# Windowed attention into a gated feed-forward block on one core: the third token tile's output product in seven block products, and a scheduler that takes every operation's place from a table

## The chip, the cores and the metric

The kernel runs on one core of one Trainium2 chip. The metric is the device time of one execution in microseconds (us). Before the change it is 309.03 us, the median of three executions (308.63 to 310.61). The profiled execution has a span of 307.2 us from its first instruction to its last.

The core's engines work at the same time, each through its own queue in order: PE multiplies matrices into the eight PSUM banks, ACT and DVE read PSUM and SBUF, POOL works on SBUF alone and issues the loads, and SP issues the stores and some copies.

## The reference, cut to what matters

```python
# q, k, v: (8, 8, 576, 64); window 64, causal
scores = (q @ k^T) / 8, masked to 0 <= i - j < 64
x = (softmax(scores) @ v).transpose(0, 2, 1, 3).reshape(4608, 512)
gate = np.maximum(x @ w_gate, 0.0)        # 512 x 1536
val = x @ w_val                           # 512 x 1536
return ((gate * val) @ w_out).astype(np.float32)   # 1536 x 512
```

## The kernel before, in words

The 4608 tokens are cut into nine tiles of 512 (tiles 0 to 8). Each tile goes through three stages.

**Attention.** For each half of the heads there is one run of 72 small matmuls ("scores", L377 and L385), four exponentials on ACT (L645), then small matmuls with the values ("values", L391), a reciprocal and a scaling on DVE (L660, L398), and a transpose on DVE (L403) that makes the tile's x.

**Hidden layer.** Tile 0 is multiplied with the weights directly (`direct_block`, L750). Tiles 1 to 8 use a scheme with seven block products for eight (`fast_hidden`, L842): the products P1 to P7 on blocks of x, on the weights and on sums of them. Per group of features and per weight (gate or value), the products P1, P6, P7 and P4 add into one and the same PSUM bank, called A, in this order. Between two of them ACT copies the bank's state to SBUF (a "snap", L851); the next product into A starts only after that copy. The copies are later added to the banks B and C by DVE (L858). ACT applies the relu (L867), and POOL multiplies gate and value into `g_sb` (L876).

**Output.** `output` (L900, its matmuls L916) multiplies a tile's `g_sb` with `wo` directly: four pieces of 128 tokens, each with three groups of four matmuls of 512 columns, an ACT copy out of PSUM (L927) and a store. `fast_output` (L955, its matmuls L1005) does it with seven block products of two halves, each half being six matmuls of 256 columns, with four sums of `g_sb` blocks on DVE (L973), three snaps on ACT (L1016), three sums on DVE (L1041) and one copy out (L1044 on ACT). `w_sums` (L939) makes the sums of `wo` blocks that this needs, once, on POOL and DVE (L950). One of its three-part sums overwrites a block of `wo`, so it has to wait for the last direct output. The constant `TF` says which tile is the first to use `fast_output`; it is 3 here, so tiles 0, 1 and 2 are done directly.

**The order of the work.** `first_part` is written out by hand: the loads that come first, 93 idle matmuls (`PADS`), and the attention of most of tile 0. The rest, `second_part`, only lists operations: each with the engines that can do it, an assumed duration, the operations it comes after, the buffers it takes and gives, and a key. `Plan.run` then plays the program through with the assumed durations; whenever an engine is free it takes the ready operation with the lowest key, and emits it. So the order in each engine's queue is settled when the program is built, and each engine then keeps to that order on the chip. The keys come from a table of constants `K` (a period per tile plus offsets per kind of operation and tile).

The plan also counts PE's instructions, since their code is loaded in blocks of 256 (`fetch`, L93): it assumes when a block is asked for and when it is there, and puts off a run of small matmuls that would have to wait for its code. `plan.at` is the count with which `second_part` starts. `fill` (L115) looks for stretches where PE would idle and books filling matmuls there, in the count and by a call of `emit`; `emit` drops what is not an operation, so no such matmul is in the program.

The loads of weights, q, k and v all go through POOL's queue (L337, L340, L347, L356), at most eight of them under way in the plan.

Of the kernel before, what the change touches and what calls it, by code (L numbers as in the profile page):

```python
# [20 lines left out]
K = {"T1": 33.417, "STEP": 29.94, "wo1": 24.303, "wo2": 136.509, "q0": 0.81, "q1": 2.61, "q10": -9.561, "q11": 1.093, "v": -0.6, "v1": 1.142, "ql": 1.41, "qt": 0.88, "qti": 4.69, "vl": 0.91, "vc": 0.04, "vm": 1.83, "e": 7.62, "gap": 3.77, "gap1": -1.003, "r": -6.21, "tn": 1.66, "xf": 4.78, "wf": -1.338, "wfj": 2.6, "sn": 2.67, "su": -2.15, "re": 17.5, "mu": -6.61, "la": -4.79, "o0": 11.594, "o0j": 20.432, "o0s": -4.369, "oo": 0.007, "os": 0.386, "oj": 4.81, "gs": -1.18, "fo": 0.015, "fi": 0.098, "fs": 4.74, "fu": 0.27, "W0": 129.92, "TF": 3, "rs": 7.037, "rv": 3.751, "rt": 4.292, "wl": 1.63, "wln": 5.389, "l0": 0.003, "l1": 4.021, "lv": 1.186, "lvs": 12.368, "wo0": 25.921, "db": -7.955, "di": 1.563, "dv": 0.646, "slack": 0.3, "d2": 3.05, "bl": 9.0, "lv0": 18.364, "d": {'0:q0': 0.808, '0:fs': 1.88, '0:la': 1.692, '1:oo': 0.058, '0:fi': 0.024, '1:qt': 3.036, '1:os': -0.226, '0:vc': -1.15, '0:tn': -0.981, '0:qt': 0.904, '0:e': -2.629, '0:sn': 0.475, '0:vm': 0.58, '0:vl': 0.514, '0:ql': 0.128, '0:fu': -2.028, '1:tn': 3.174, '0:re': 0.858, '1:ql': -1.577, '0:xf': -0.14, '0:su': 0.053, '0:gap': 0.391, '0:r': -2.955, '0:oo': -0.042, '0:os': 0.025, '1:vm': 0.483, '1:fo': -0.017, '0:q1': 0.357, '1:sn': 0.632, '0:oj': -0.104, '0:qti': -0.947, '0:gs': -0.096, '0:fo': -0.029, '2:xf': -3.116, '1:oj': -0.851, '1:fu': -1.619, '1:gs': -1.956, '1:vl': 3.671, '1:fs': -1.692, '1:q0': -0.44, '1:re': 17.838, '1:qti': -0.251, '2:vl': -1.63, '1:xf': 0.54, '2:v': 0.897, '2:e': 3.091, '1:vc': -0.626, '2:gap': 1.519, '1:mu': -1.202, '2:oj': 1.272, '2:os': -0.152, '1:gap': -2.068, '1:su': 1.664, '1:q1': 0.09, '1:la': -0.927, '2:fu': -0.861, '2:q0': -1.678, '2:su': -3.121, '1:v': 0.703, '1:r': 0.099, '2:tn': 0.263, '2:mu': -0.767, '2:qti': -1.435, '2:sn': 0.235, '2:qt': 0.357, '3:re': -0.971, '3:su': 1.85, '2:gs': 0.316, '2:vc': -0.222, '2:fi': 0.018, '3:fs': 2.376, '2:oo': -0.024, '3:gs': -0.499, '2:ql': 2.087, '2:re': 1.781, '2:vm': -0.346, '2:la': -0.408, '3:fo': 0.105, '3:qt': -1.251, '3:qti': -0.756, '3:fi': 0.003, '3:r': 4.605, '4:tn': 4.441, '4:fo': 0.176, '3:sn': 1.86, '3:v': -0.191, '3:gap': 0.067, '3:q1': -1.861, '4:v': -2.381, '3:fu': -1.0, '3:e': -2.398, '3:ql': 0.244, '3:q0': -0.417, '4:ql': 1.859, '4:qti': -0.846, '3:oo': 0.017, '3:oj': -1.455, '3:mu': 5.549, '3:vl': -0.094, '3:la': -1.756, '3:os': 0.07, '4:qt': -2.162, '5:v': 2.345, '5:e': -6.12, '5:gap': -0.396, '4:re': 16.126, '4:r': -3.179, '4:os': 0.054, '4:q0': -0.903, '4:gap': -1.023, '4:fu': -1.144, '5:vm': 1.185, '4:fi': -0.029, '4:vm': 1.023, '4:la': 2.23, '4:vl': 0.037, '5:tn': -1.009, '5:r': -1.653, '5:fu': 0.073, '5:re': 3.794, '4:q1': 1.992, '4:sn': 1.164, '4:xf': -1.831, '5:fi': -0.019, '4:mu': 1.169, '4:oj': 1.089, '5:qti': -1.537, '5:fo': -0.021, '5:xf': -1.396, '5:gs': -0.82, '5:mu': -2.334, '5:vc': -0.566, '5:oo': 0.002, '5:q0': -0.047, '4:vc': 0.378, '5:qt': -1.506, '4:fs': 0.072, '5:ql': -0.361, '5:oj': 0.91, '5:fs': -0.532, '5:q1': -0.028, '4:oo': -0.002, '5:la': 0.275, '6:oo': -0.051, '6:vl': -1.345, '6:v': 0.087, '7:vc': 2.102, '6:os': 0.034, '7:fo': -0.026, '6:tn': -1.475, '6:gap': -1.442, '6:xf': 3.27, '6:fi': -0.035, '6:fo': -0.054, '6:fu': -0.179, '6:qt': 0.741, '7:tn': -0.289, '7:vl': -0.177, '6:ql': -0.604, '7:re': 9.431, '7:fi': 0.019, '7:xf': -0.992, '6:vc': -0.932, '7:sn': -0.018, '6:e': 6.905, '6:q1': 1.236, '7:ql': -0.482, '7:e': -4.862, '7:qt': 1.66, '6:mu': -0.73, '7:gap': 0.823, '6:oj': 0.303, '6:q0': 0.231, '6:r': 2.887, '7:su': 1.478, '7:gs': -0.403, '7:q0': -0.079, '7:q1': -0.303, '7:vm': -1.095, '6:gs': -0.02, '7:mu': -0.49, '7:fs': 1.309, '7:la': -0.048, '7:os': 0.117, '7:qti': -1.407, '7:r': -0.97, '7:fu': -0.866, '6:re': 0.021, '6:la': 0.896, '7:oo': -0.007, '6:sn': 0.915}}  # L21
# [5 lines left out]
class Op:  # L27


    def __init__(self, name, key, engines, fn, after, take, give, dma):  # L30
        self.small = 0
        self.count = 0
        self.opens, self.closes = None, False
        self.name = name
        self.key, self.engines, self.fn = key, engines, fn
        self.take, self.give, self.dma = take, give, dma
        self.left = len(after)
        self.feeds = []
        self.ready = dict.fromkeys(engines, 0.0)
        self.end = None  # L40
        self.on = None


class Plan:
# [12 lines left out]
    def __init__(self, free, queue, pools):  # L57
# [4 lines left out]
        self.taken = {}  # L62
        self.open = []
        self.filled = []
# [50 lines left out]
    def fill(self, o, t, emit):  # L115
        if t - self.free["PE"] < 0.7:
            return
        free = [(self.taken[id(h[n])], h[n]) for pool, h, names in o.take if "bank" in pool for n in names]
        free += [(x[0], x[2]) for pool in ("bank", "bo") for x in self.pools[pool]]
        if free or self.open:  # L120
            since, bank = min(free, key=lambda x: x[0]) if free else (0.0, self.open[-1]["b"])
            since = max(self.free["PE"], since + 0.1)
            n = int((t - 0.25 - since) / 0.165)
            if n > 0:
                self.fetch(2 * n, since, 0.165 * n, True)
                self.filled.append((since, n, t, o.name))
                emit((bank, bool(free)), n)

    def finish(self, o, e, t, dur):
        if e == "PE":  # L130
            if o.opens is not None and o.opens in self.open:
                self.open.remove(o.opens)
            if o.opens is not None and not o.closes:
                self.open.append(o.opens)
# [29 lines left out]
    def grab(self, o, e, t):  # L164
# [7 lines left out]
        for holder, names, items in got:  # L172
            for name, item in zip(names, items):
                self.pools[self.home[id(item[2])]].remove(item)
                self.taken[id(item[2])] = item[0]
# [37 lines left out]
    def run(self, emit):  # L213
# [7 lines left out]
        while left:  # L221
# [7 lines left out]
            while moved:  # L229
                moved = False  # L230
                for e in ("PE", "ACT", "DVE", "POOL", "SP"):
# [13 lines left out]
                    if e == "PE":  # L245
                        self.fill(o, begin, emit)
# [9 lines left out]
def kernel(  # L256
# [255 lines left out]
    def second_part():  # L512
# [562 lines left out]
        def emit(o, e):  # L1075
            if not isinstance(o, Op):
                return
# [46 lines left out]
```

## Time and profile before

| | |
|---|---|
| Time, median of three (lowest to highest) | 309.03 us (308.63 to 310.61) |
| Span of the profiled execution | 307.2 us |
| PE busy | 297.1 us, 97% |
| DVE, POOL, ACT busy | 246.2, 229.8, 213.0 us |
| Granted TensorE clock, mean | 0.999 |
| Matmuls of the direct output (L916) | 144 of 512 columns |
| Matmuls of the seven-product output (L1005) | 504 of 256 columns |

The difference between the median time and the profiled span, 1.83 us, lies outside the first and last instruction. Durations of instructions below are those of this one execution. A matmul's shown end is a modelled one: matmuls follow each other faster than their shown durations. The profile calls an engine's wait "issue" when it ended with nothing that the profile shows.

### The profile page before, as it was taken

What the parts mean: (1) busy time and instruction counts of PE and PEld (TensorE: products, weight loads), DVE (VectorE), ACT (ScalarE), POOL (GpSimd) and SP (SyncE); (2) the same over time, 40 slices, a digit from 0 to 9 for tenths busy, and PEclk for the clock granted to TensorE, in tenths of its full rate; (3) what the DMA queues carried; (4) which work ended last, traced back from release to release, by engine and by line L of the source; (5) the groups of instructions that cost most, each with busy time, mean ns of one, the idle gap of its engine ahead of it and who ended that gap; (6) DMA issues with size and microseconds to landing.
All of it is one profiled execution on the core that took longest, in us unless ns stands there. A gap on an engine that the chain in (4) does not pass through costs nothing.

```text
span 307.2 us, 11254 instructions
## 1 busy us (share of the span) xinstructions
PE 297.1 (97%) x4772; PEld 240.2 (78%) x4772; DVE 246.2 (80%) x422; ACT 213.0 (69%) x414; POOL 229.8 (75%) x233
## 2 busy tenths in 40 slices
PE   7889999998999999999999999999999999999995
PEld 5475845786757886777888888888888888888884
DVE  5858997988963997887989988878896789595762
ACT  4445335897768787788778786778687886878721
POOL 8696957998999899999189954995479157938520
PEclk9999999999999999999999999999999999999999
DMA  7999999983249953996694194674112011201033
GB/s 219 187 190 206 196 194 198 202 169 22 19 78 150 183 99 75 139 182 136 123 72 82 34 165 120 48 166 37 54 36 69 6 38 37 68 0 36 1 121 120
DMA packets 59074, 32.87 MB, mean 107 GB/s; under 512 B 39440, under 2 KB 53392, under 8 KB 59024
## 3 DMA queue, kind: packets, MB, share of 16 engines
q0 software_dynamic: 46672, 18.29, 51.1%
q1 hardware_dynamic: 12208, 13.80, 14.2%
q8 instruction: 37, 0.61, 0.8%
q14 instruction: 13, 0.11, 0.1%
q10 hardware_dynamic: 144, 0.07, 0.1%
HBM read 37.75 MB, written 9.44 MB: 154 GB/s over the span
## 4 chain that ended last, share of the span: by engine, by line
PE 85%; DMA 8%; POOL 3%; issue 2%; DVE 1%; ACT 0%; ACTq 0%; DVEq 0%; POOLq 0%
PE bank L842 48%; PE bank L1005 18%; PE bank L916 8%; PE bank L391 4%; PE bank L750 3%; DMA wo<-in_moe_w_out_dram 3%; DMA wv<-in_moe_w_val_dram 3%; DMA k<-in_k_dram 2%; PE bank L385 2%; PE bank L377 1%; POOL vs L791 1%; POOL v L356 1%; POOL q L347 0%; POOL k L347 0%; DVE xw L398 0%
## 5 line engine op out<-in xcount | busy, mean ns | idle before, releaser
L876 POOL TENSOR_TENSOR g_sb<-pr,pr 128x512 f16<-128x512 f32 x96 | 121.6, 1283 | 47.7 <-ACT pr L889 16.5
L858 DVE TENSOR_TENSOR pr<-bank,pr 128x512 f32<-128x512 f32 x144 | 92.6, 678 | 24.7 <-PE bank L842 21.9
L851 ACT COPY pr<-bank 128x512 f32<-128x512 f32 x144 | 79.9, 590 | 30.2 <-PE bank L842 27.9
L842 PE MATMUL bank<-xt,vs 128*128 128x256 f16 x384 | 56.7, 273 | 0.0
L842 PE MATMUL bank<-xt,us 128*128 128x256 f16 x384 | 56.2, 273 | 0.0
L867 ACT ACTIVATE pr<-pr 128x512 f32<-128x512 f32 x72 | 45.4, 639 | 5.9 <-DVE pr L858 5.5
L842 PE MATMUL bank<-xt,wg 128*128 128x256 f16 x288 | 42.8, 273 | 0.0
L842 PE MATMUL bank<-xt,wv 128*128 128x256 f16 x288 | 42.7, 273 | 0.0
L842 PEld LDWEIGHTS <-us 128*128 128x128 f16 x384 | 37.0, 98 | 6.5 <-issue 0.2
L842 PEld LDWEIGHTS <-vs 128*128 128x128 f16 x384 | 37.2, 98 | 4.7
L645 ACT ACTIVATE p<-bank 128x512 f16<-128x512 f32 (+1 forms) x68 | 35.7, 592 | 6.7 <-PE bank L385 6.5
L916 PE MATMUL bank<-wo,g_sb 128*128 128x512 f16 x144 | 35.9, 380 | 0.3 <-DMA wo<-in_moe_w_out_dram 0.3
L356 POOL DMA_DIRECT2D v<-in_v_dram x40 | 34.9, 883 | 0.5 <-issue 0.5
L889 ACT ACTIVATE pr<-bank 128x512 f32<-128x512 f32 x48 | 27.1, 601 | 6.7 <-PE bank L842 5.0
L842 PEld LDWEIGHTS <-wg 128*128 128x128 f16 x288 | 27.7, 98 | 4.7
L842 PEld LDWEIGHTS <-wv 128*128 128x128 f16 x288 | 28.1, 98 | 4.2
L1005 PEld LDWEIGHTS <-g_sb 128*128 128x128 f16 x288 | 27.9, 98 | 3.4
L1005 PE MATMUL bank<-wo,g_sb 128*128 128x256 f16 x216 | 28.4, 273 | 0.0
L398 DVE TENSOR_TENSOR xw<-bank,r 128x448 f16<-128x448 f32 (+2 forms) x45 | 25.8, 575 | 1.5
L403 DVE STREAM_TRANSPOSE xt<-xw 128x512 f16<-128x512 f16 (+2 forms) x38 | 25.0, 668 | 0.5 <-ACT xw L506 0.3
L1005 PEld LDWEIGHTS <-ss 128*128 128x128 f16 x216 | 21.0, 98 | 2.5
L916 PEld LDWEIGHTS <-g_sb 128*128 128x128 f16 x144 | 13.5, 98 | 11.3 <-issue 0.3
(95 smaller groups left out, 389.4 us busy)
## 6 DMA issues: line engine op xcount, KB each, us to landing
out_dram<-pr SPq DMA_DIRECT2D x35, 256.0 KB, 2.4
k<-in_k_dram POOLq DMA_DIRECT2D x15, 288.0 KB, 7.5
q<-in_q_dram POOLq DMA_DIRECT2D x15, 288.0 KB, 7.1
v<-in_v_dram POOLq DMA_DIRECT2D x32, 128.0 KB, 6.4
v<-v SPq DMA_DIRECT2D x12, 132.0 KB, 2.6
v<-v SPq DMA_DIRECT2D x24, 66.0 KB, 2.3
wg<-in_moe_w_gate_dram POOLq DMA_DIRECT2D x6, 256.0 KB, 6.6
wv<-in_moe_w_val_dram POOLq DMA_DIRECT2D x6, 256.0 KB, 7.9
```

Source lines behind the costliest of these rows:

```text
L356: nc.gpsimd.dma_start(v16s[b % 2][lo:hi, g, :, 0:64], v[b, :, 64 * g - 64 + lo:64 * g - 64 + hi].rearrange("h p d -> p h d"))
L398: nc.vector.tensor_tensor(x, blocks_of(to, n)[:, :, 0:D].rearrange("p s (c e) -> p s e c", e=2), r[:, :, :, None].to_broadcast([128, n, 2, ...
L403: nc.vector.transpose(xt[:, 2 * hh:2 * hh + 2, c0:c0 + n].rearrange("p e (s c) -> p s e c", c=32), x)
L645: nc.scalar.activation(pp[g][:, 0:n].rearrange("p n c -> p (n c)"), st[g][:, 0:64 * n], ACT.Exp, scale=scale)
L842: nc.tensor.matmul(slot[to][:, HT * m:HT * m + HT], w[:, kk, 128 * m:128 * m + 128], x[:, kk], start=(first and m == 0 and kk == 0), stop= ...
L851: lambda e, hold=hold, slot=slot: nc.scalar.copy(hold["x"], slot["A"]),
L858: nc.vector.tensor_tensor(hold["x"], slot[to], hold["x"], ADD)
L867: lambda e: nc.scalar.activation(hold["x"], hold["x"], ACT.Relu), after=[o])
L876: lambda e: VEC[e].tensor_tensor(gh[:, fs:fs + 2, h], pair(a["x"]), pair(b["x"]), MUL),
L889: lambda e, hold=hold, slot=slot, i=i: nc.scalar.activation(hold["x"], slot["A"], ACT.Copy if i else ACT.Relu),
L916: nc.tensor.matmul(bank["b"][:, 0:c1 - c0], gs[t % 2][:, f, 128 * sub:128 * sub + 128], wo[:, f, c0:c1], start=(j == 0 and i == 0), stop=( ...
L1005: nc.tensor.matmul(bank[to][:, HD * m:HD * m + HD], a[:, f, 128 * m:128 * m + 128], b[:, f], start=(first and m == 0 and f == 0), stop=(f ...
```

## The change

`TF` goes from 3 to 2, so tile 2 is done by `fast_output` too, and `w_sums` waits for the direct outputs of two tiles. The durations and start times that the plan assumes are set to new values. `fill` and what it needs are taken out. After all 1618 operations are listed, each one's key is replaced by a number from a table `PLACES`. Everything else in `K` stays; it now matters only for what reads it beside the keys.

```diff
-K = {..., "TF": 3, ...}
+K = {..., "TF": 2, ...}
+PLACES = [int(n) / 100 for n in """
+-1900 -468 778 272 1607 821 1292 824 3602 2123 12645 -290 -1508 6258 ...
...
@@ fetch
-                begin += max(0.4, min(6.5, self.queue["q"] - begin), min(2.0, self.queue["sp"] - begin))
-                come.append(begin + 2.4 + K["slack"])
+                begin += max(0.7, min(4.0, self.queue["q"] - begin), min(2.0, self.queue["sp"] - begin))
+                come.append(begin + 1.2)
...
-    def fill(self, o, t, emit):
-        if t - self.free["PE"] < 0.7:
-            return
...
@@ second_part
-        plan = Plan({"PE": 14.3 - FRONT, "ACT": 16.2 - FRONT, "DVE": 16.8 - FRONT, "POOL": 13.2 - FRONT, "SP": 3.0},
-                    {"q": 16.4 - FRONT, "sp": 3.0},
...
+        plan = Plan({"PE": 15.35, "ACT": 16.95, "DVE": 17.55, "POOL": 13.6, "SP": 3.0},
+                    {"q": 16.6, "sp": 3.0},
...
-        plan.at = 428 + 2 * 72
-        plan.asked, plan.got, plan.come = 2, 1, [12.1 - FRONT, 18.8 - FRONT]
+        plan.at = 428 + 2 * PADS
+        plan.asked, plan.got, plan.come = 2, 1, [7.9, 16.9]
...
-                                        after=[turns[b - 1, name, hh]] if b > 1 else [], dma=(0.59, 0.40, "q"))
+                                        after=[turns[b - 1, name, hh]] if b > 1 else [], dma=(0.59, 0.41, "q"))
...
-                                              dma=(0.26 * (part[2] - part[1]) / 128, 0.22, "q"))
+                                              dma=(0.26 * (part[2] - part[1]) / 128, 0.28, "q"))
...
-            run = op("scores", key, pe(0.0081 * 8 * n + 0.0268 * n), lambda e: score_run([st[g] for g in range(G)], items),
+            run = op("scores", key, pe(0.0083 * 8 * n + 0.0268 * n), lambda e: score_run([st[g] for g in range(G)], items),
...
-            a = op("values", key, pe(0.031 * m), run, after=after, take=[("bank", to, ("b",))], give=gives)
+            a = op("values", key, pe(0.02 + 0.031 * m), run, after=after, take=[("bank", to, ("b",))], give=gives)
...
+                if f0 < 4 and kind == "v" and c0 < 2 * U:
+                    ops[-1].ready["PE"] = 17.95
...
+        assert len(PLACES) == len(plan.all)
+        for o, place in zip(plan.all, PLACES):
+            o.key = place
         end = plan.run(emit)
```

As built, PE's program changes from 144 to 96 matmuls of the direct output and from 504 to 588 of the seven-product output. The other counts that change: ACT 417 to 419 instructions, DVE 424 to 429, POOL 238 in both. The order within every queue changes from the first operation of `second_part` to near the end.

More of the change, by code (lines that the diff above doesn't have):

```diff
@@ L113, in fetch @@
         return t
-    def fill(self, o, t, emit):
-        if t - self.free["PE"] < 0.7:
-            return
[L118 to L127, printed above, removed]
     def finish(self, o, e, t, dur):
         if e == "PE":
[L131 to L134, printed above, removed]
             dur += self.TURN * ((o.small > 0) != self.small)
@@ L920, in output @@
                         before[0].count = 4
-                        before[0].opens, before[0].closes = bank, j == NJ - 1
                         mine += before
```

19 lines of the change are left out of this document (5 added, 14 removed), and 66 rows, old and new, of the table PLACES.

## The prediction

> **What bounds the kernel now.** I read the page first, then the busy time by stretches, then the chain that ended last, then the order of time around each gap on PE.
>
> From the page:
>
> ```profile
> PE 297.1 (97%) x4772; PEld 240.2 (78%) x4772; DVE 246.2 (80%) x422; ACT 213.0 (69%) x414; POOL 229.8 (75%) x233
> PE 85%; DMA 8%; POOL 3%; issue 2%; DVE 1%; ACT 0%; ACTq 0%; DVEq 0%; POOLq 0%
> q8 instruction: 37, 0.61, 0.8%
> ```
>
> PE sets the end: 97% busy, 85% of the chain. So the time falls only by what leaves PE or by what PE waits. Where it waits, by stretches (length, then PE, PEld, DVE, ACT and POOL busy with their instructions, clock, DMA share, GB/s):
>
> ```profile
> 15.00:50.00 35.00, 33.22 (x557) 22.78 (x556) 28.01 (x60) 15.63 (x35) 26.60 (x35) 1.00 1.37 198
> 50.00:150.00 100.00, 98.37 (x1671) 74.88 (x1671) 83.03 (x135) 78.16 (x149) 91.06 (x90) 1.00 0.86 127
> 150.00:303.00 153.00, 153.00 (x2237) 134.82 (x2236) 124.08 (x203) 111.68 (x208) 101.42 (x87) 1.00 0.32 63
> ```
>
> After 150 us PE never stops. Before that it is idle for 1.78 and 1.63 us. Matmul ends are modelled, so I size the gaps from start to start instead. From the chain (start, length, what), the true spacings:
>
> ```profile
> 57.59 0.86 PE bank L916 x4
> 74.65 3.93 PE bank L842 x36
> 176.77 1.31 PE bank L1005 x12
> ```
>
> A 512-column matmul takes 0.86/4 = 0.215 us, a 256-column one 3.93/36 = 1.31/12 = 0.109. The gaps in order of time:
>
> ```profile
> 16.64 0.33 PE L750 MATMUL bank<-xt,wv 128*128 128x192 f16 x2
> 17.97 1.33 PE L750 MATMUL bank<-xt,wv 128*128 128x192 f16 x14 [1.01 <-DMA wv<-in_moe_w_val_dram]
> ...
> 29.67 1.26 PE L750 MATMUL bank<-xt,wg 128*128 128x128 f16 x16 [0.20 <-DVE xt L403]
> ...
> 50.13 1.02 PE L916 MATMUL bank<-wo,g_sb 128*128 128x512 f16 x4 [0.33 <-DMA wo<-in_moe_w_out_dram]
> ...
> 70.31 0.21 PE L391 MATMUL bank<-v,p 128*32 128x65 f16 x3
> ...
> 71.55 0.82 PE L391 MATMUL bank<-v,p 128*32 128x65 f16 x69 [1.03 <-issue]
> ...
> 149.13 0.20 PE L385 MATMUL bank<-qT,kT 32*128 32x64 f16 x2 [0.31 <-issue]
> ```
>
> From start to start, less the stream itself, they are worth: x transposes at 15.1 us, 0.30; the first value weights, 1.17; x transposes at 29.1 and 29.7, 0.57; exponentials at 41.9, 0.40; `wo` at 50.1, 0.52. Together 2.96 us before 50 us. Then 0.52 around 53 and 66 us, 1.24 at 70.3, 0.15 at 94, 0.50 at 148.6: 2.41 us. The two called "issue" I take for PE's code: 9544 PE instructions in blocks of 256 make 37, the packets of queue q8.
>
> **The change part by part.**
>
> *Seven products for eight in tile 2.* Out go 12 groups of four wide matmuls at 0.86: 10.32 us. In come 14 groups of six narrow ones at 0.655: 9.17. PE: **-1.15 us**. DVE gets four block sums (1.11, 0.96, 0.95, 0.95) and three sums at 0.68: +6.0 us, less about 1.0 for value copies that move to ACT and POOL. ACT swaps four copies for three snaps and one copy. This lies beside PE: DVE is busy 83 of 100 us between 50 and 150 us, POOL 91, so 17 and 9 are open. Without that cover, up to 6.0 us of later sums would hold PSUM banks and PE would wait for them. The overwriting sum of `wo` moves from after tile 2's direct outputs to after tile 1's; in the built order 25 groups of the hidden layer alone (25 x 0.437 = 10.9 us) stand on PE between the last of these and the first product that reads it. I cost it at nothing. The stores stay in number and size on SP's queue.
>
> The row above stands against a rule of the Trainium skill, page "TensorE: Matmul & The Clock Gate", section "Back-to-back issue gap": in a sustained stream of weight load and matmul pairs, a 512-column matmul takes about 131 ns and a 128-column one 81. An estimate from that page puts 256 columns near 98 ns, so the exchange would cost 84 x 98 - 48 x 131 ns, some +1.9 us instead of -1.15. The trace's 215 and 109 ns do not agree with it.
>
> *The stretch to 50 us.* In the new order PE runs, behind the first two gate blocks, the small scores (0.47 us) and a third gate block (0.66) before it asks for the value weights. The third block needs x transposed, done at 17.57, so PE starts it near 17.65 and ends at 18.31. By then it has done three blocks and the scores, 2.43 us of work; before, it had done 18.31 - 15.03 less its gaps of 0.30 and 1.17, so 1.81: 0.62 gained. Between tile 0's values and the 128-column blocks that need their transpose now stand four blocks (2.6 us) for two (1.3); the row of DVE steps between took 1.9 (28.07 to 29.94): the 0.57 goes. Between scores and values of tile 1 two more blocks (1.3) stand: the 0.40 goes. That is 1.59. But the last third of `wo` landed at 50.09, behind the same loads. PE would ask for it at 49.61 - 1.59 plus 0.87 of work put ahead of it (28 value matmuls, one product), 48.9. If the landing stays, PE waits 1.2 and only the 0.87 is kept. In POOL's queue five sums of 1.16 stand ahead of that load for seven, so it can be issued up to 2.3 earlier, though its queue serves in order; I take 0.4 earlier: **-1.3** (bounds 0 and -2.96).
>
> *50 to 150 us.* The plan's count of PE instructions starts 42 further on (93 pads for 72), and `fill` no longer books code for matmuls never emitted. Both put its block borders where the program's are, so it can keep small runs off them. I take 0.8 of the 1.74 at "issue" and none of the other gaps: **-1.4** (bounds 0 and -2.41).
>
> *What the new order adds.* One more stretch of small matmuls on PE: +0.1, as one change of kind cost 0.09 before. Then the handing over of bank A: from the last issue of a product to the next one into A pass 0.21 until ACT starts (0.04 behind the shown end, which is 0.17 behind the stream), 0.59 for the copy (L851), 0.04 to release: 0.84. By PE's order and the spacings above, none of the 144 hand-overs before has less than 1.09 of other work between; now three have less than 0.9 (0.44, 0.71, 0.87, all near tile 1's first group), which lacks 0.40 + 0.13. So +0.5. Within 1.2 stand 19 for four. Where ACT is in another copy of 0.59, one that has 1.09 lacks 0.34; 16 x 0.34 = 5.4 is the whole; the four before lost nothing visible. I take an eighth: +0.7 (bounds 0 and 5.4). Behind a waiting product stands everything on PE.
>
> *Sum:* -1.15 - 1.3 - 1.4 + 0.1 + 0.5 + 0.7 = -2.55. On the profiled span 307.2 this gives 304.7; with the 1.83 outside it as in the median, **306.5 us**. The last 3.8 us (last matmul at 303.4, then copy and store) stay.
>
> **The rivals.**
>
> *A, all gaps close.* -1.15 - 2.4 - 2.0 + 0.6 = -4.95: about 304.1; with a part of it, 304.5. For it: every gap before 150 us has a cause that the new figures name (17.95 for the value weights, the count). Against: the `wo` landing and the tight hand-overs.
>
> *B, gaps only move.* `wo` lands as before or later, the code blocks meet other small runs: -1.15 + 0.6, 308.5. For it: loads fill the queue up to 50 us at 198 GB/s, and PE's order cannot hasten them.
>
> *C, slower: the hand-overs of bank A decide.* 19 stand within 1.2 and 37 more within 1.32; with a copy ahead they need 0.84 + 0.59 = 1.43. All hit would be 19 x 0.34 + 37 x 0.12 = 10.9. Two thirds of it, 7.2, against gains of 3.85, gives 309.0 - 3.85 + 0.6 + 7.2 = 313.0. It decides from 3.3 us on, a third of them. For it: PE has not one idle moment after 150 us now, so the new order can only lose there beyond the exchange. Against: ACT is busy 112 of 153 us there.
>
> *D, the exchange does not pay.* If shown durations were the cost (273 ns narrow, 380 wide), 84 x 0.273 - 48 x 0.380 = +4.7 replaces -1.15: 312.4. Against it stand the spacings on the chain. The Trainium skill's 131 ns above would give 309.5, by that page ("TensorE: Matmul & The Clock Gate") alone.
>
> **How the numbers follow.** My forecast 0.42 (own range 305.2 to 308.0), A 0.25, B 0.20, C 0.11, D 0.02. A measurement of this kernel tells about 1% from no change: below 305.9 is faster, above 312.1 slower. A and 0.13 of the forecast make 0.38 faster; half of C and D, 0.06 slower; the rest 0.56. The range 303.8 to 310.2 leaves out the far end of A and C.
>
> **What would show it.** In the output stage 96 matmuls of 0.215 and 588 of 0.109. No gap at the first value weights over 0.6 us, none at the 128-column blocks; the `wo` wait larger than 0.52. Code gaps of 1.24 and 0.50 gone or small. New: short PE waits on ACT's copies in the hidden layer after 150 us. I am wrong if PE stops for more than 3 us after 150 us, if a gap over 1 us stands at a code block again, or if the span falls under 302.

## The result: about 2 us slower

| | before | after |
|---|---|---|
| Time, median of twenty (lowest to highest) | 308.23 us (307.03 to 310.61) | 310.39 us (308.99 to 314.35) |
| Ratio, 95% interval | | 1.0067 (1.0047 to 1.0087) |
| Span of the profiled execution | 307.2 us | 308.0 us |
| That execution's own time | | 309.76 us |
| A second profile of the same kernel: span, own time | 306.5, 308.42 us | 308.3, 309.96 us |

The changed kernel is slower by 0.67%, some 2.07 us. The two spans of before differ by 0.7 us, so the profile that the prediction was made from was one of the longer ones. The mean spans, 306.85 and 308.15, are 1.3 us apart. About half of the rest is that the profiled executions of the changed kernel lie 0.05 and 0.6 us under their medians, and the second of before 0.2 over 308.23.

### The profile page after: what moved, and what is told of

Its sections match the earlier page's. It is cut to its first block, busy times and chain, and to the rows that moved or that the text cites. A ratio compares the mean times of both kernels' runs of the same rounds, so it can differ in the third digit from the quotient of the medians.

```text
span 308.0 us, 11241 instructions
## 1 busy us (share of the span) xinstructions
PE 297.1 (96%) x4808; PEld 244.0 (79%) x4808; DVE 251.9 (82%) x427; ACT 215.7 (70%) x416; POOL 228.8 (74%) x233
## 4 chain that ended last, share of the span: by engine, by line
PE 86%; DMA 7%; DVE 2%; issue 2%; ACT 1%; POOL 1%; SPq 0%; ACTq 0%; POOLq 0%; DVEq 0%
PE bank L888 46%; PE bank L1050 21%; PE bank L962 7%; PE bank L436 4%; DMA v<-in_v_dram 3%; PE bank L430 3%; DMA v<-v 2%; PE bank L422 2%; PE bank L794 2%; DMA vs<-in_k_dram 1%; PE bank L497 1%; DVE us L837 0%; DVE qT L398 0%; DVE kT L398 0%; POOL us L837 0%
## 5 line engine op out<-in xcount | busy, mean ns | idle before, releaser
L904 DVE TENSOR_TENSOR pr<-bank,pr 128x512 f32<-128x512 f32 x144 | 94.1, 683 | 19.6 <-ACT pr L897 9.2
L897 ACT COPY pr<-bank 128x512 f32<-128x512 f32 x144 | 81.3, 587 | 24.1 <-PE bank L888 20.6
L888 PE MATMUL bank<-xt,vs 128*128 128x256 f16 x384 | 56.1, 273 | 0.0
L888 PE MATMUL bank<-xt,us 128*128 128x256 f16 x384 | 56.0, 273 | 0.0
L689 ACT ACTIVATE p<-bank 128x512 f16<-128x512 f32 (+1 forms) x68 | 36.9, 594 | 10.1 <-PE bank L430 10.1
L888 PE MATMUL bank<-xt,wg 128*128 128x256 f16 x288 | 42.1, 273 | 0.3 <-ACT pr L897 0.3
L888 PE MATMUL bank<-xt,wv 128*128 128x256 f16 x288 | 41.9, 273 | 0.0
L888 PEld LDWEIGHTS <-us 128*128 128x128 f16 x384 | 37.2, 98 | 5.1
L888 PEld LDWEIGHTS <-vs 128*128 128x128 f16 x384 | 36.9, 98 | 4.7
L1050 PEld LDWEIGHTS <-g_sb 128*128 128x128 f16 x336 | 32.6, 98 | 4.4 <-issue 0.5
L935 ACT ACTIVATE pr<-bank 128x512 f32<-128x512 f32 x48 | 28.0, 600 | 11.0 <-PE bank L888 10.5
L1050 PE MATMUL bank<-wo,g_sb 128*128 128x256 f16 x252 | 32.8, 273 | 0.3 <-issue 0.3
L888 PEld LDWEIGHTS <-wg 128*128 128x128 f16 x288 | 27.7, 98 | 5.1 <-issue 0.5
L888 PEld LDWEIGHTS <-wv 128*128 128x128 f16 x288 | 28.0, 98 | 3.8
L1050 PEld LDWEIGHTS <-ss 128*128 128x128 f16 x252 | 24.5, 98 | 2.9
L962 PE MATMUL bank<-wo,g_sb 128*128 128x512 f16 x96 | 23.7, 380 | 0.0
L398 DVE STREAM_TRANSPOSE qT<-q 128x576 f32<-128x576 f32 x16 | 19.8, 1249 | 3.9 <-DMA q<-in_q_dram 3.3
```

The source lines that it names most:

```text
L689: nc.scalar.activation(pp[g][:, 0:n].rearrange("p n c -> p (n c)"), st[g][:, 0:64 * n], ACT.Exp, scale=scale)
L888: nc.tensor.matmul(slot[to][:, HT * m:HT * m + HT], w[:, kk, 128 * m:128 * m + 128], x[:, kk], start=(first and m == 0 and kk == 0), stop= ...
L897: lambda e, hold=hold, slot=slot: nc.scalar.copy(hold["x"], slot["A"]),
L904: nc.vector.tensor_tensor(hold["x"], slot[to], hold["x"], ADD)
L935: lambda e, hold=hold, slot=slot, i=i: nc.scalar.activation(hold["x"], slot["A"], ACT.Copy if i else ACT.Relu),
L962: nc.tensor.matmul(bank["b"][:, 0:c1 - c0], gs[t % 2][:, f, 128 * sub:128 * sub + 128], wo[:, f, c0:c1], start=(j == 0 and i == 0), stop=( ...
```

## The profile after

The page of the changed kernel: PE's busy time with its share and instructions (and PEld, DVE, ACT, POOL), and the chain that ended last by engine.

```profile
PE 297.1 (96%) x4808; PEld 244.0 (79%) x4808; DVE 251.9 (82%) x427; ACT 215.7 (70%) x416; POOL 228.8 (74%) x233
PE 86%; DMA 7%; DVE 2%; issue 2%; ACT 1%; POOL 1%; SPq 0%; ACTq 0%; POOLq 0%; DVEq 0%
```

PE still sets the end. DVE has 5.7 us more (6.0 less about 1.0 were costed). The same three stretches as in the prediction, with the same columns:

```profile
15.00:50.00 35.00, 32.46 (x555) 22.65 (x539) 28.51 (x59) 17.32 (x37) 27.11 (x36) 1.00 1.36 196
50.00:150.00 100.00, 98.46 (x1737) 77.90 (x1735) 87.70 (x141) 78.22 (x147) 90.31 (x89) 1.00 0.81 118
150.00:303.00 153.00, 152.43 (x2234) 134.62 (x2232) 124.47 (x203) 112.67 (x209) 100.74 (x87) 1.00 0.37 68
```

PE's idle time is now 2.54 us before 50 us (1.78 before), 1.54 to 150 us (1.63), and 0.57 after it, where there was none. Who PE waited for (line, releaser, us in total, times, longest), first from 15 to 76 us, then from 150 to 303 us:

```profile
PE bank L430 <- issue: 1.7, 2, 1.2
PE bank L422 <- ACT pr L806: 0.7, 1, 0.7
PE bank L436 <- issue: 0.7, 1, 0.7
PE bank L436 <- DMA v<-v: 0.5, 1, 0.5
PE bank L888 <- ACT pr L897: 0.3, 1, 0.3
...
PE bank L1050 <- issue: 0.3, 1, 0.3
PE bank L436 <- issue: 0.3, 1, 0.3
```

The waits for `wv` and `wo` are gone, and so are the two waits at "issue" that stood at 70.3 and 148.6 us: the list has only one wait of the values at "issue" up to 76 us, and from 75 to 150 us PE never stops in this profile.

```profile
75.00:150.00 75.00, 75.00 (x1247) 60.75 (x1246) 66.11 (x105) 59.65 (x113) 67.54 (x66) 1.00 0.74 102
```

In their place stand five waits at "issue" elsewhere. L430 and L436 are the scores' and values' small matmuls (L385 and L391 before), L888 the hidden products (L842), L1050 the seven-product output (L1005). The chain around them (start, length, what):

```profile
17.28 0.15 PE bank L430 x19
17.42 1.21 issue
18.63 0.28 PE bank L430 x12
...
44.96 0.09 PE bank L430 x11
45.04 0.50 issue
45.54 0.59 PE bank L430 x53
...
50.45 0.32 PE bank L436 x23
50.77 0.69 issue
51.46 0.19 PE bank L436
...
161.00 0.32 PE bank L1050 x2
161.33 0.31 issue
161.63 0.60 PE bank L1050 x4
...
184.32 0.50 PE bank L436 x45
184.82 0.26 issue
185.08 0.24 PE bank L436 x6
```

PE stops inside a run of like matmuls and goes on with the next of the same run (at 161 us inside the six matmuls of an output product, behind a run of values), and the profile shows no operand or bank that was missing. Counted from the program's start, every one of these places is PE instruction 188 to 190 of a block of 256: the borders of the code blocks. The blocks are the 37 packets of queue q8, of 16 KB each. A view of the DMA of 43.0 to 43.2 us shows one of them among the loads:

```profile
q8 instruction: 1, 0.02, 30.4%
```

It began at 43.06 us, and PE went on behind the border at 45.54 us. In both profiles of the changed kernel the five blocks that made a gap were first used 2.24 to 2.56 us after their transfer began; every other block had at least 2.87 us. The transfer is asked for, as far as the starts let it be seen, 280 PE instructions ahead of the border. In 512-column matmuls (two instructions and 0.215 us each) that is 30 us of work; in values or scores, at 10.0 and 8.3 ns a matmul, 1.2 to 1.4 us. Between this point and the packet's start pass 0.1 to 3.6 us after 65 us, but 3 to 6 us between 12 and 51 us, where loads fill the queues. So a border is reached before its block when most of the 280 instructions before it are small matmuls, and sooner where the transfer starts late.

The Trainium skill, page "Runtime: NRT & Kernel Launch", section "Instruction fetch mechanics", has the same blocks of 16 KiB and 256 instructions, fetched through DMA while the block before runs, and calls the cost of a border mostly hidden. The block size agrees. Hidden it is not at every border: five of the 37 here cost 3.8 us in sum, start to start.

To set the whole of PE in order, I took each spacing between the starts of two matmuls, valued it at the median of its pair of kinds, and called the rest excess, put into the stretch in which the spacing begins (no matmul's record is missing in these four profiles):

| us | at medians | excess to 15 us | 15 to 50 | 50 to 150 | from 150 |
|---|---|---|---|---|---|
| before, two profiles | 286.25 | 1.70, 1.79 | 3.90, 3.29 | 6.10, 5.89 | 3.90, 3.91 |
| changed, two profiles | 285.53 | 2.18, 1.73 | 4.27, 4.64 | 6.05, 5.95 | 4.61, 5.01 |

The stream itself is 0.72 us shorter. Waits are 0.9 us longer before 50 us and 0.9 us longer after 150 us, on the means, and as long as before in between. The code gap of 0.86 us near 50 us begins at 50.58 us in one profile of the changed kernel and at 49.53 in the other, so it is counted on both sides of that border; with the border at 52 us, the means are 1.2 us more before it and 0.3 us less from there to 150.

## The experiments

Theory: the table puts small runs where the chip has not yet loaded their code, because the plan takes a block to be usable 1.2 us after its transfer begins (2.4 and a slack of 0.3 before). Beside it a second limit: copies in SP's queue ("v moves", L664) that hold the values of tile 2 until about 64.5 us. (A batch, below, is one entry of the first index of q, k and v.) Rivals: the new order is too tight for the banks and copies, or the exchange itself does not pay.

**The changed kernel again.** No edit.

> The changed kernel once more, for a second profile. Three theories of the 2 us that it loses. Code: PE's instructions come in blocks of 256, PE needs the next block 280 instructions after it is asked for, and the new order puts runs of small matmuls where the block is not there yet; the plan takes a block to be usable 1.2 us after its load begins, and the traces show 2.2 to 2.6. Then the five gaps of the first profile (17.2, 44.9, 50.6, 161.1, 184.6 us, together 3.8 us) stand again at the same instructions (number 188 to 190 in their block), 3 to 4.5 us together, and nowhere else. Hand-overs (PE waits on copies of bank A and on banks): gaps on ACT's and DVE's release, over 3 us together, spread after 50 us. Load (the four sums and three adds more on DVE): PE waits for DVE and POOL around 115 to 150 us. Time 310.4 for all three.

310.01 us, ratio 1.0070 (1.0044 to 1.0096). The same five code gaps at the same instructions: 1.07, 0.59, 0.86, 0.36 and 0.94 us; the v wait is 1.12. PE's waits from 15 to 150 us, the longer ones:

```profile
PE bank L430 <- issue: 1.3, 2, 0.9
PE bank L436 <- DMA v<-v: 1.0, 1, 1.0
PE bank L436 <- issue: 0.7, 1, 0.7
...
PE bank L436 <- DVE pr L904: 0.4, 1, 0.4
```

The code gaps belong to the order and not to chance; their sizes vary, and the wait on DVE, at 98 us, was not in the first profile.

**Borders moved: 109 and 79 pads.**

```diff
-    PADS = 93
+    PADS = 109
...
-        plan.at = 428 + 2 * PADS
+        plan.at = 428 + 2 * 93
```

> The changed kernel with 109 idle matmuls at the start for 93, and the plan's count left as it is, so the order of every operation stays and only the borders of the code blocks move, by 32 instructions to earlier work. The 16 idle matmuls (0.43 us) fit into PE's wait of 0.65 us at 3.7 us. Code: from the trace's times, with each block's delay as it was, the gaps fall from 3.8 to about 1.5 us (0.9 at 17 us, 0.6 at 48.5; none at 45, 161 and 185): 2 to 3 us faster than the changed kernel, 307.5 to 308.4. Hand-overs and load: order and work are the same, so within 0.4 us of the changed kernel, 310.4.

> The same the other way: 79 idle matmuls for 93, order kept, borders of the code blocks 28 instructions later. Code: the gaps grow by about 1 us (1.1 at 17.6, 2.1 at 43.6, 0.7 at 49.7, 0.7 at 91.6, 0.8 at 182.3), so 311 to 312. Hand-overs and load: as the changed kernel, 310.4, or up to 0.3 less for 14 matmuls less.

313.07 us, ratio 1.0156 (1.0126 to 1.0186), and 315.2 us, 1.0230 (1.0192 to 1.0267). With 109 the gaps near 44, 49, 161 and 185 us went, as they should when borders move; the one at 17 us stayed, as expected. But others came (0.80 at 24.1 for a weight load, 1.38 at 163.5 for code), and PE stood 1.56 us for the v moves at 62.9 and 1.94 us for DVE at 98.1. With 79 one code gap was 2.50 us. Both times lie above every range that was written down, and some 1.7 us of each is a stretch at half clock behind the longest stop (last section). That borders make the gaps is borne out; that this order would be fast with other borders is not.

**Tile 2 with eight products again, table kept.**

```diff
-K = {..., "TF": 2, ...}
+K = {..., "TF": 3, ...}
...
-        for o, place in zip(plan.all, PLACES):
+        places = ...   # tile 2's 20 direct operations spread over the places of its products
+        for o, place in zip(plan.all, places):
```

> The changed kernel with tile 2's output done directly again (12 groups of 0.86 us for 14 of 0.655), all other operations with their places from the table, the direct groups at the places of the products. Code and hand-overs: PE's work grows by 1.15 us, the code blocks behind 115 us shift by 72 instructions, so the two gaps at 161 and 185 us may go or others come: 309.5 to 312.5. Load: DVE loses 6 us of sums between 115 and 150 us, and the loss goes: 308 to 309.

327.27 us, ratio 1.0628, far above both ranges. PE waited for copies and sums over 115 to 235 us. It says nothing of the exchange: a part cannot be swapped while the table stays. The exchange is read from the trace instead: the output stages' matmuls fill 87.86 us from start to start before and 86.74 after (87.94 and 86.62 in the second profiles).

**Loads moved, code moved, both.** The plan's order is kept; single operations are moved behind another. On PE 115, 121 and 127 are output groups of tile 0, 684 is half an output product of tile 3 (the expectations of late_only and late_2 below call it a hidden block), 1100 a value run of tile 6; the others are stores, v moves and loads.

```diff
-        end = plan.run(emit)
+        order = []
+        end = plan.run(lambda o, e: order.append((o, e)))
+        for n, behind in MOVES: ...   # operation n right behind operation behind
+        for o, e in order:
+            emit(o, e)
+# loads_mended
+MOVES = [[510, 321], [124, 325], [134, 124], [119, 134]]
+# code_mended
+MOVES = [[115, 131], [121, 189], [127, 121], [684, 809], [1100, 870]]
+# both_mended: code_mended's and loads_mended's
```

> The changed kernel with its order kept and four DMA issues moved: three of tile 0's last stores go behind the first four v moves of batch 2 on SP, and one q load of batch 3 goes behind the two value loads that these moves wait for on POOL. Theory (two absolute times hold PE in the first 65 us: the arrival of its code blocks, and the landing of the v moves): the wait in the values of tile 2 that ended at 64.5 us in both runs of the changed kernel (0.68 and 1.12 us) goes, the moves land some 2 to 4 us earlier, the code gaps near 17, 44, 50, 161 and 184 us stay; 0.7 to 1.1 us less than the 310.0 us of the unchanged kernel, so 308.9 to 309.4 us, ratio to before about 1.003 to 1.005. Rival (what is freed comes back as another wait, since the queues are interlocked): 309.7 to 310.4 us, ratio 1.006 to 1.008, with a new gap of 0.5 us or more between 60 and 75 us.

> The changed kernel with its order kept and five matmul groups moved: before the small runs that stood at the code borders near 44, 50, 161 and 184 us one or two groups of 512 columns are put (0.4 to 1.7 us more work ahead of the border, the instruction numbers of the borders unchanged). Theory: these four gaps (0.59, 0.86, 0.36 and 0.94 us in the repeat of the changed kernel) go; of the first two nothing is won, since PE then stands longer for the v moves until 64.5 us (a wait of 2 to 2.6 us there instead of 0.7 to 1.1); of the last two 0.9 to 1.3 us are won: 308.7 to 309.2 us, ratio to before 1.002 to 1.004. Rival (code is not what costs, or the gaps turn up at the next border): no change, 309.7 to 310.4 us. Rival (the v moves are no limit): all four gaps are won, 307.2 to 307.6 us.

> Both sets of moves in one kernel. Theory of the two limits: the sum is more than its parts, since the first two code gaps can be won only when the v moves land earlier: 3.2 to 3.9 us less than the changed kernel, 306.1 to 306.9 us, ratio to before 0.993 to 0.997; PE passes the values of tile 2 near 61 us. Rival (parts add): 307.6 to 308.4 us. Rival (the freed time turns into other waits): over 309 us.

loads_mended: 309.58 us, ratio 1.0048 (1.0023 to 1.0072), between the two ranges; the interval overlaps that of the repeat, so a gain is not told apart. The v wait is gone, the code gaps stand. PE's waits from 50 to 76 us in it (lines are 4 higher than above, L440 is the values):

```profile
PE bank L440 <- issue: 1.0, 1, 1.0
PE bank L892 <- ACT pr L901: 0.3, 1, 0.3
```

code_mended: 309.61 us, 1.0037 (1.0019 to 1.0055), where 308.7 to 309.2 was expected. Three of the four gaps went; the one at 161 us turned up in the group put ahead (0.67). As the theory said of the first two, nothing was won: PE waited for the v moves until 64.8 us (1.16) and for banks before that (0.43, 0.51 and 0.46).

both_mended: 310.73 us, 1.0068 (1.0047 to 1.0088), where 306.1 to 306.9 was expected. All four gaps and the v wait were gone, but the next block's transfer began only at 54.96 us, and PE stopped 0.43 and 1.28 us in the scores of tile 2. Behind that the granted clock fell (columns as above; the seventh number is the clock):

```profile
52.00:57.00 5.00, 4.00 (x74) 2.11 (x73) 4.83 (x11) 2.25 (x4) 2.89 (x4) 1.00 1.67 204
57.00:61.00 4.00, 3.63 (x30) 2.58 (x30) 2.95 (x4) 2.17 (x4) 3.90 (x5) 0.57 1.61 198
61.00:65.00 4.00, 3.66 (x34) 3.13 (x33) 2.48 (x6) 3.25 (x7) 2.75 (x3) 1.00 1.00 201
```

From 57.8 to 61.0 us every matmul of 256 or 512 columns took twice its spacing, which cost 1.7 us. So the sum of the parts failed: one mended border meets the next, and half clock came behind two stops close together.

**The table taken away.** The new durations and the exchange stay, the keys come from the old formulas.

```diff
-        assert len(PLACES) == len(plan.all)
-        for o, place in zip(plan.all, PLACES):
-            o.key = place
```

> The changed kernel without the table: the new durations and the seven products for tile 2 stay, the places come from the formulas with the old constants, as in the kernel before. The plan's own end is 310.2 us of its clock against 301.2 with the table. Theory (the plan's forecast is good to 3 us or so, and the table is what fits the order to the new durations): 314 to 321 us, ratio 1.02 to 1.045, with PE waits spread over the whole span. Rival (the table's order is what loses time on the chip, by being tight): at or below the changed kernel, 306 to 310 us.

323.72 us, ratio 1.0514 (1.0473 to 1.0555). The plan's own end was 9.0 us later than with the table; the chip lost 13.3 us against 310.39. Against the old formulas the table is worth that much to the new durations. How an order made for the measured arrival of the code would do, this run does not show.

**More room in the queue.** Both q and k loads of batch 3's first heads go behind the value loads of batch 2, in place of the first pair of loads_mended, `[510, 321]`.

```diff
+# loads_2
+MOVES = [[512, 327], [510, 512], [124, 325], [134, 124], [119, 134]]
+# both_2: code_mended's and loads_2's
```

> The moves of both_mended, and besides the two hh 0 loads of batch 3 (k at 46.5 us, q at 50.3 us there) go behind all value loads of batch 2 on POOL. What both_mended showed: its four code gaps and the v wait were gone, but the next code block's transfer began at 54.96 us (53.5 in code_mended), 1.28 us too late for the scores of tile 2 at 56.06 us, and the granted clock was half for 3.4 us behind that, which costs 1.7 us. Theory (code blocks come late because they stand behind loads already queued): with 1.4 us less of loads queued at 47 us this block's transfer begins at 53.5 us or sooner, the gap at 56 us and the half clock go: 310.7 less 1.3 less 1.7 gives 307.4 to 308.2 us, ratio to before 0.997 to 1.001. Rival (the code's delay has nothing to do with these loads): gap and half clock stay, 310.3 to 311.1 us, ratio 1.006 to 1.009.

> The changed kernel with only the DMA issues moved: three of tile 0's last stores behind the first four v moves on SP, as in loads_mended, and both hh 0 loads of batch 3 behind all value loads of batch 2 on POOL. Theory: as loads_mended (309.6 us, 0.4 to 0.8 us below the changed kernel), and the code block that ended the gap near 49.8 us (transfer at 48.6 us, asked for near 43 us, before either load is issued) doesn't come sooner, so the gaps near 17, 44, 50, 161 and 184 us stay: 309.0 to 309.8 us, ratio 1.002 to 1.006. Rival (the loads of batch 3 are what delays this block): the gap at 50 us shrinks by 0.5 us or more and the time goes to 308.4 to 308.9 us.

both_2: 309.76 us, ratio 1.0053 (1.0033 to 1.0073). The transfer that began at 54.96 us now began at 54.05; the gap at 56 us and the half clock were gone. Yet the time missed its range of 307.4 to 308.2: waits for banks stood at 62.0 (0.83) and 98.3 us (0.74), and the code gap near 185 us came back (0.79). loads_2: 310.09 us, 1.0067 (1.0047 to 1.0086), above its 309.0 to 309.8; gaps as expected, and 1.50 us at 184.

**Only after 150 us.**

```diff
+# late_only
+MOVES = [[684, 814], [1100, 949], [1101, 1100], [1102, 1101]]
+# late_2
+MOVES = [[684, 814], [1100, 870]]
+# late_loads: late_2's and loads_mended's
```

> The changed kernel with its order kept up to 158 us; of what follows, two PE groups are moved: the first half of a hidden block of tile 3 (at 161 us) behind the next three 256 column groups, the second value run of tile 6 (at 184 us) behind the next three, with its reciprocal and norm. Each border of code then comes 1.3 to 1.5 us of work later than the gap in it, where code_mended had 0.9 to 1.1. Theory (code blocks that land too late for the order are a loss of their own after 150 us, where no landing of a load holds PE afterwards): both gaps go (0.36 to 0.47 and 0.43 to 1.5 us in the runs so far), nothing replaces them, and PE's wait time after 150 us falls to 0.3 us or less; 308.6 to 309.3 us, ratio to before 1.002 to 1.005. Rival (freed time comes back as waits for copies and banks, since the order is tight): 309.7 to 310.4 us, with new gaps of 0.8 us or more in sum after 165 us.

> The changed kernel with two PE groups moved and nothing else: the half hidden block at 161 us behind the next three 256 column groups, the second value run of tile 6 at 184 us behind the next two groups (0.44 and 0.65 us), its reciprocal and norm staying in their places on DVE. Theory (code gaps after 150 us are a loss of their own): the gap at 161 us falls to 0.3 us or less and the one at 184 us (0.43 to 1.5 us so far) to 0.5 us or less, no new wait over 0.3 us after 165 us, 0.8 to 1.3 us won less 0.2 us for the extra changes between large and small runs: 309.0 to 309.6 us, ratio to before 1.003 to 1.005. Rival (no gain, as in late_only): 309.8 to 310.4 us.

> The moves of late_2 and the DMA moves of loads_mended in one kernel. Theory (gains far apart in time add): loads_mended lay 0.4 us under the repeat of the changed kernel, late_2 should lie 0.6 to 1.0 us under it: 308.4 to 309.0 us, ratio to before 1.001 to 1.004; no wait for the v moves near 64 us, gaps after 150 us 0.6 us or less in sum. Rival (each freed stretch is eaten by the next wait): 309.5 us or more.

310.23 us, 1.0051 (1.0026 to 1.0076); 310.07 us, 1.0051 (1.0027 to 1.0075); 309.9 us, 1.0043 (1.0018 to 1.0068). The rivals were right on the times. In late_only the code gaps fell from 1.30 to 0.27 us, but the reciprocal and norm moved along made PE wait 0.61 us. In late_2 and late_loads the code gaps fell to 0.29 and 0.25, while PE stood 1.06 and 1.34 us at 98 us. That wait, as late_loads' chain shows it:

```profile
87.37 8.33 DMA q<-in_q_dram
...
96.90 1.24 DVE qT L402
98.13 0.53 DVE pr L908
98.66 0.04 issue
98.71 0.31 PE bank L440 x13
```

A q load of batch 4, issued at 87.4 us, lands at 95.70. DVE's queue stands 2.9 us at its transposes, the sum that releases a bank stands behind them, and PE behind the sum. The same wait was 0.53 us in the repeat and none in the first profile. In late_loads, which has no v wait, what PE won before 98 us is taken here. In late_2, where nothing before 158 us was moved, the wait shows how far this place varies from one execution to another; one profile of each is too few to tell the two apart.

**The loads made small.** In both kernels the eight q and k loads of batches 2 and 3 bring one eighth of their columns.

```diff
-        nc.gpsimd.dma_start(nat[name, hh], heads_of(b, name, hh))
+        n = S // 32 * D // (8 if b in (2, 3) else 1)
+        nc.gpsimd.dma_start(nat[name, hh][:, 0:n], heads_of(b, name, hh)[:, 0:n])
```

> The changed kernel, its order unchanged, with the eight q and k loads of batches 2 and 3 (issued at 35 to 61 us) cut to one eighth of their columns: scores of these batches are of other data. Theory (code blocks and v moves are late because they stand behind queued loads): the blocks whose transfers began at 41.9 and 48.2 us in the repeat begin at least 1 us earlier, the gaps at 44 and 50 us (0.59 and 0.86 us) and the v wait at 63.4 us (1.12 us) go, those at 17, 161 and 184 us stay: 310.0 less 2.6 gives 307.0 to 307.9 us, ratio to before 0.996 to 1.000. Rival (the block's delay is in its own queue): the gaps at 44 and 50 us stay and only the v wait goes, 308.8 to 309.4 us. Rival (the order is so tight that other waits take their place): over 309.4 us.

> The kernel before with the same eight loads cut to one eighth. Theory: its order has no code gap between 20 and 65 us and no v wait, so it has less to win: the w_out landing at 49.6 us (0.49 us) and perhaps the code gap at 70.3 us (1.2 us): 306.4 to 307.7 us, ratio 0.994 to 0.999, a gain smaller than that of the changed kernel by 1 us or more. Rival (loads cost both orders the same): 2.3 to 2.9 us less, 305.2 to 305.8 us.

The changed kernel: 308.5 us, ratio 1.0016 (0.9995 to 1.0037). The kernel before: 308.34 us, 1.0011 (0.9997 to 1.0025). So the changed kernel won 1.5 us against its repeat, the kernel before nothing (306.4 to 307.7 was expected), and the two are level. PE's waits from 15 to 150 us in the changed kernel with small loads (lines are 1 higher than in the changed kernel):

```profile
PE bank L431 <- issue: 1.9, 2, 1.2
PE bank L423 <- ACT pr L807: 0.4, 1, 0.4
PE bank L889 <- ACT pr L898: 0.3, 1, 0.3
PE bank L437 <- DVE pr L905: 0.3, 1, 0.3
```

The v wait and the code gap at 50 us are gone: the block asked for at 43.7 us began 2.8 us later (4.5 in the repeat), the next 1.1 (4.3). The gap at 44 us stayed (0.90): its block, asked for at 37.3 us, still began 5.0 us later; that loads which were not cut stood ahead of it is likely, but not shown. The expected 307.0 to 307.9 was missed by that gap and by 0.65 and 0.96 us of code gaps after 150 us.

**Small loads and the late moves together.**

> The changed kernel with the eight q and k loads of batches 2 and 3 cut to one eighth (scores of these batches are of other data) and the two PE moves of late_2. Theory (what the exchange wins is held back by landings of loads and by code blocks, and by nothing else): the late moves now add to the small loads, 308.5 less 0.3 to 1.0, so 307.5 to 308.2 us, under the 308.3 us of the kernel before with the same loads; the q load of batch 4, which is not cut, still makes the DVE queue and then PE wait at 97 us. Rival (gains never come through): 308.3 us or more.

308.1 us, ratio 0.9992 (0.9974 to 1.0009), span 306.0 against 306.3 of the kernel before with small loads. PE's excess from 150 us on fell from 5.32 to 4.35 us. The time lies at the upper end of what was expected and 0.2 us under 308.34, which is not told apart from it. The wait at 97 us that was expected did not come; a v wait of 0.81 at 62 us did.

**The kernel before again.**

> The kernel before, unchanged, for a second profile of it. Theory (a gap stands where a block's border meets a small run, and its size follows when that block's transfer begins): the waits stand in the same places as in its first profile (first value weights 16.7 us, code at 70.3 and 148.6 us, the w_out landing at 49.6 us), each within 0.5 us of 1.2, 1.2, 0.5 and 0.5 us; no code gap in any other place; span 306.5 to 307.9 us, time 307.9 to 308.3 us, ratio 0.999 to 1.001. Rival (code gaps fall anywhere, as the queues happen to stand): other places or a sum of code gaps over 3 us.

> The kernel before, unchanged, for a second profile. Theory: waits in the same places as in its first profile (wv near 16.7 us, w_out near 49.6, code near 70.3 and 148.6 us), each within 0.5 us of 1.2, 0.5, 1.2 and 0.5 us, no code gap elsewhere; span 306.5 to 307.9 us. Rival (code gaps fall anywhere): other places or over 3 us of code gaps.

The first gave 308.02 us (ratio 0.9978, 0.9950 to 1.0007); its profiled execution ran at a granted clock of 0.76, and its gaps are not compared. The second, one execution of 308.42 us with a span of 306.5, waited from 15 to 150 us for (the two longest):

```profile
PE bank L750 <- DMA wv<-in_moe_w_val_dram: 1.1, 1, 1.1
PE bank L385 <- issue: 0.8, 1, 0.8
```

The gaps at 16.5 us (1.28) and at the scores' border near 148 us (1.01, 0.5 before) stand again. The code gap of 1.21 at 70.3 us and the `wo` wait of 0.49 do not: the transfer of the block at 70 us began 1.5 us after it was asked for, not 3.75.

## Why the prediction was wrong, step by step

It said 306.5 us (303.8 to 310.2) and 0.06 for slower by over 1%; the change came out 0.67% slower, just over the range at 310.39 and within it in the repeat.

- *Seven products, -1.15:* right. The output stages shrank by 1.12 us. PE's whole stream shrank by 0.72, since the changed order puts other kinds next to each other.
- *The Trainium skill's 131 ns (page "TensorE: Matmul & The Clock Gate", section "Back-to-back issue gap"):* the trace kept to 0.216 and 0.110 us, and rival D fell.
- *DVE's +6.0 us, at nothing:* 5.7 us came. In the changed kernel DVE made PE wait only at 98 us, 0.53 us in one of two profiles, and there because its queue stood for a load.
- *The stretch to 50 us, -1.3:* failed; its waits grew by 0.9 us. The gaps for the transposes at 29 us (0.57) and the exponentials (0.40) closed, as it said, and so did the `wo` wait, which it expected to grow. The step that failed is the small scores put ahead of the value weights, with 0.62 gained: it put their code at nothing. Those scores cross a border after 27 of 40 matmuls (biases included), and their block, whose transfer began at 16.08 us, was usable at 18.63. A wait of 1.17 for `wv` became one of 1.37 for code in the same place (1.07 in the second profile). Two more code gaps came, 0.67 and 0.86 us near 45 and 50 us, and a wait for banks (0.89 us at 38 us, 0.67 in the second profile), since a relu on ACT that frees one stood behind a copy of v values whose load landed at 37.43 us.
- *50 to 150 us, -1.4:* failed; 0.0. The two code gaps that it wanted gone are gone: from 52 to 150 us neither profile of the changed kernel has one. The plan's count does put the borders where the chip has them. What failed is that closing them would shorten the stretch. In their place stand 0.51 us for a copy of bank A at 61 us (before has 0.18 and 0.43 at 53 us), 0.68 and 1.12 us for the v moves at 64 us, and in the second profile the 0.53 us at 98. The v moves were put at nothing; the stores were weighed by number and size, not by their place ahead of the moves on SP's queue (loads_mended, with three stores and a load put behind, has no v wait). Besides, 1.21 of the 1.74 us to be won was one execution's: the second profile of before has no gap at 70 us.
- *Code, the term that is missing in both:* a border at the right place helps only with the right arrival. The diff's `begin + 1.2` for `begin + 2.4 + K["slack"]`, 4.0 for 6.5 as the longest queueing, and 16.9 us as the arrival of the block at 17 us, were in front of me, and I costed the count and not these numbers. Measured: 2.24 to 2.56 us from the transfer's start, up to 6.0 of queueing, and PE going on at 18.63 and 18.11 us. So "it can keep small runs off them" held against a plan that believes the code to be there 1.0 to 1.4 us too early.
- *The new order, +0.1 + 0.5 + 0.7:* the size was near (0.9 us more from 150 us on), the cause was not, so that is luck. Of the tight hand-overs of bank A one shows, the 0.51 us at 61 us, in every profile of this order. After 150 us none: what came there is code, 0.36 to 0.94 us at 161 and 184 us.
- *Rivals:* B, "gaps only move", had the mechanism, with its "loads fill the queue", but not its price: moved gaps came out larger. C, the slower side, had the wrong place.
- *What was to show it:* the counts and spacings of the output's matmuls, the closed gaps at the 128-column blocks and the closed code gaps at 70 and 149 us came as said; a larger `wo` wait and short waits on ACT's copies after 150 us did not. A gap over 1 us at a code block was named as the sign that I am wrong, and it stood there (1.37). The span's floor of 302 and 3 us of stops after 150 us were not touched.
- *The base:* the profiled 307.2 and the median of three, 309.03, were both high; later medians of before are 308.0 to 308.3. That the repeat's 310.01 falls inside the range is owed to this base.

What is shown: the code gaps by their instruction numbers and packets in both profiles of the changed kernel; that with the loads of batches 2 and 3 made small the difference of the two kernels is gone, together with the v wait and the code gap at 50 us, while the code gaps at 17, 44, 161 and 184 us stand. What stays open: that the table puts small runs at these borders because the plan takes the code to be there too early is read from the diff, and no run tests it. A version that beats the kernel before was not found. None of the mended orders did, and whether a plan with the measured 2.4 us, and a table made anew for it, would, was not tried.

## What to carry to other kernels

Where PE issues small matmuls, count instructions as well as time: here 280 of them are gone in 1.2 us, and the next block of code took up to 2.56 us plus its place in the DMA queues. A plan that is made tighter must be priced by the assumptions it relaxes, each of them, and not only by the waits it is meant to close. Before a gap is booked as winnable, see it in a second profile.

## What the runs showed of the hardware

Half clock can follow a stop of PE. Stops of 1.94 us (109 pads), 2.50 us (79 pads), 2.74 and 4.9 us (no table), a pair of 0.43 and 1.28 us within 2.4 us (both_mended) and five of 0.28 to 1.08 us within 5 us (no table) were followed by 2.8 to 3.4 us in which every matmul of 256 or 512 columns took double. The traces' records of the granted clock have 0.5 for 3.41 us each time, beginning between 0.1 us before and 1.2 us after PE went on; each such stretch cost about 1.7 us. A stop of 1.99 us at 63 us (79 pads) did not do it, nor did five of 0.34 to 1.01 us within 6 us from 165 us on (tile 2 direct), so the length of the stop alone does not decide it. The Trainium skill, page "TensorE: Matmul & The Clock Gate", section "What's actually happening", has a free-running window of 3413 ns behind the gate: the 3.41 us of these stretches agree. The Trainium skill's table on the same page, in "Why this matters for your kernels", warns of idle gaps over about 3 us; here 1.94 was enough, and the measurement decides.
